# Two decode attentions on one core: the first K block ahead of B's query weights, and TensorE's loop rotated

## The chip, the cores and the metric

The kernel runs on one core of one Trainium2 chip. The metric is device time in microseconds (us) of one execution; lower is better. Before the change it takes 672.21 us (median of 3 runs, 672.11 to 673.36). One execution was also profiled: it took 671.92 us, and its trace spans 670.2 us from the first to the last instruction.

## The reference

Two independent one-token decode attentions, A and B, have the same sizes: D = 512, 32 heads of 128, a cache of 8192 keys and values per head, all bfloat16. Their outputs are put side by side.

```python
# for each of A and B; x is [1, 1, 512]
q = (x @ wq).reshape(1, 1, 32, 128).transpose(0, 2, 1, 3)
scores = einsum("bhqd,bhkd->bhqk", q, k_cache) * 128 ** -0.5
p = softmax(scores, axis=-1)
o = einsum("bhqk,bhkd->bhqd", p, v_cache)
y = o.transpose(0, 2, 1, 3).reshape(1, 1, 4096) @ wo      # [1, 1, 512]
# out = concatenate([y of A, y of B], axis=-1)
```

Each cache is 64 MiB, and there are four. Each of the four weight matrices is 4 MiB. Each of these bytes is read once.

## The kernel before, in words

**Groups.** Four heads make a group, so A has groups 0 to 7 and B has groups 8 to 15 (N = 16). K of a group (8 MiB) fills one of two SBUF buffers, `kn[0]` and `kn[1]`, in turn. V of a group (8 MiB) fills the only V buffer, `vn`. The query weights `wq` of A and of B (4 MiB each) also lie in `vn`, one half each, before V of group 0 overwrites them.

**One group.** VectorE multiplies K by the query, broadcast over the keys, in four blocks h = 0 to 3 (L307, `plan_mul`). For each block TensorE adds up groups of products with 16 matmuls against the identity into PSUM (L461, `scores`), and VectorE reduces these to 64 scores per partition (L312, `plan_sr`). After block 3 come the maximum (L319), two small matmuls on TensorE that turn it and broadcast it (L499, L502), and four exponentials on ScalarE (L335). PV is 256 matmuls (L490) and a small one for the sum of the exponentials (L483); VectorE scales the result (L341, L342).

**Queries.** The query of A is 32 matmuls (L277) once `wq` of A has landed, and that of B 32 more once `wq` of B has landed. ScalarE copies the results to `qbc`. In the code before, TensorE runs both sets before its loop begins.

**The loads.** SyncE (SP) issues every large load from one queue, in the order in which the program lists them: `wq` of A, `wq` of B, K of 0, K of 1, V of 0, K of 2, V of 1, K of 3, and so on. A load that must wait for a buffer holds up everything behind it. V of 0 waits for the last query matmul (`q_done`). V of n waits for PV of n-1 (`pv_done`). K of n+2 waits until the fourth score block of group n has been added up by TensorE (`red_done(n, 3)`). At the end come `wo` of A, the first half of `wo` of B, V of 15 in two parts, and the rest of `wo` of B in five smaller pieces, which land last.

**TensorE's program.** All engines but TensorE run straight code. TensorE has a real loop over r = 0 to 16 (L475), whose body is made of branches on r. In the order of the code: score blocks 0 to 2 of group r, in two copies, one for each K buffer (L470, L476); for r = 16 alone the middle part, that is the relayout, the output product of A, and the first half of that of B (L478); for r > 0 PV of group r-1 (L480); for r < 16 block 3 of group r and the two small matmuls (L496), and back to the top (L475). After the loop follows the last part: the rest of B's output product, and its turn into rows (L419, L436). A part that a round does not use is jumped over. Register waits (`_Stepped`) count up round by round.

So from one round to the next TensorE does: blocks 0 to 2 of group r, PV of r-1, block 3 of group r, small matmuls, then blocks 0 to 2 of r+1.

Of the kernel before, what the change touches and what calls it, by code (L numbers as in the profile page):

```python
# [11 lines left out]
P = 128  # L12
# [11 lines left out]
class _Plan:  # L24
# [15 lines left out]
    def op(self, eng, fn, ctr=None, needs=(), inc=1):  # L40
        for m in needs:
            self.wait(eng, m)
        self.prog[eng].append((fn, ctr, inc))
        if ctr is None:
            return None
        ctr.n += inc
        return ctr, ctr.n


def _emit(e, items):  # L50
    for fn, ctr, k in items:
        if fn is None:
            e.wait_ge(ctr.sem, k)
        elif ctr is None:
            fn(e)
        else:
            fn(e).then_inc(ctr.sem, k)
# [18 lines left out]
def bass_concat_heads__mha_block_cached__gqa_block_cached__decode_kernel(  # L76
# [16 lines left out]
    wqs = [A_wq, B_wq]  # L93
    wos = [A_wo, B_wo]
    NA = 2
# [7 lines left out]
    G = 4  # L103
    HP = P // G
    T = Sk // HP
    assert T == 256
    GA = H // G
    N = NA * GA
    NB = 4
    HT = T // NB  # L110
    DW = 512 // HT
    VT = 192
# [7 lines left out]
    with ExitStack() as st:  # L120
# [3 lines left out]
        def sb(name, shape, dt):  # L124
            return ec(nc.sbuf_tensor(name, shape, dt))

        kn = [sb("k%d" % i, [P, T, Dh], BF16) for i in range(2)]
        vn = sb("vn", [P, T, Dh], BF16)
# [3 lines left out]
        wq_buf = [vflat[:, a * WQ:(a + 1) * WQ] for a in range(NA)]  # L132
# [5 lines left out]
        pt = sb("pt", [P, T, G], BF16)  # L138
# [4 lines left out]
        ones_f = sb("ones_f", [P, P], F32)  # L143
        ident = sb("ident", [P, P], BF16)
        ident_f = sb("ident_f", [P, P], F32)
        m1 = sb("m1", [P, 1], F32)
        gm = sb("gm", [1, G], F32)
        gmx = sb("gmx", [1, P], F32)
        negb = sb("negb", [P, N], F32)
        rsum = sb("rsum", [P, G], F32)  # L150
# [10 lines left out]
        def ps(name, shape):  # L161
            return ec(nc.psum_tensor(name, shape, F32))

        rps = ps("rps", [P, 2, 512])
        acc = ps("acc", [P, 512])
        mtp = ps("mtp", [P, 512])
        bmp = ps("bmp", [P, 512])
        misc = ps("misc", [P, 512])
        yps = [ps("yps%d" % i, [P, 512]) for i in range(2)]

        pl = _Plan()
        op, wait = pl.op, pl.wait

        def ctr(name):
            return _Ctr(nc, st, name)

        s_x = ctr("s_x")
        s_w = [ctr("s_w%d" % a) for a in range(NA)]
# [3 lines left out]
        s_v, s_v2 = ctr("s_v"), ctr("s_v2")  # L182
# [3 lines left out]
        c_red, c_sum, c_pv, c_gx, c_bc = ctr("c_red"), ctr("c_sum"), ctr("c_pv"), ctr("c_gx"), ctr("c_bc")  # L186


        def red_done(n, h):
            return c_red, NB * n + h + 1  # L190
# [13 lines left out]
        def dma(eng, dst, src, c, needs=()):  # L204
            return op(eng, lambda e: e.dma_start(dst, src), c, needs, inc=16)  # L205


        def const(fn, needs=()):
# [12 lines left out]


        x_in = [dma("ACT", xrow[0:1, a, :], xs[a][0], s_x) for a in range(NA)][-1]
        wq_in = [dma("SP", wq_buf[a], wqs[a].rearrange("(p c) n -> p (c n)", p=P), s_w[a])
                 for a in range(NA)]
        k_in, v_in = {}, {}

        def load_k(n):
            a, i = divmod(n, GA)
            src = ks[a][0, G * i:G * (i + 1)].rearrange("h (p t) d -> (h p) (t d)", p=HP)  # L230
            k_in[n] = dma("SP", kflat[n % 2], src, s_k[n % 2],
                          [red_done(n - 2, NB - 1) if n >= 2 else None])
# [8 lines left out]
        def load_wob(g, need=None):  # L241
# [9 lines left out]
                dst = wo_sb[1][:, h0:h0 + n, :]  # L251
            wob_in.append(dma("SP", dst, src, s_wob[g], [need]))


        def xmm(e):
            r = None
            for a in range(NA):
                for c in range(C):
                    k = (a * C + c) * HP
                    r = e.matmul(misc[:, k:k + HP], xrow[0:1, a, c:D:C], ones_bf[0:1, 0:HP],  # L260
                                 start=True, stop=True)
            return r
        m = op("PE", xmm, c_pe, [x_in, i_pool])
# [2 lines left out]
        y_free = [x_ready, x_ready]  # L266
        qbc_ready = {}
        q_done = None
        for a in range(NA):
            for j in range(GA // 4):  # L270
                def qmm(e, a=a, j=j):
                    r = None
                    for hh in range(G):
                        for c in range(C):
                            w = wq_sb[a][:, c, 16 * j * Dh:16 * (j + 1) * Dh].rearrange(
                                "p (i h d) -> p i h d", h=G, d=Dh)[:, :, hh, :]
                            r = e.matmul(  # L277
                                yps[j % 2][hh * HP:(hh + 1) * HP, :].rearrange("p (i d) -> p i d", d=Dh),
                                xb[:, a, c, :], w, start=(c == 0), stop=(c == C - 1))
                    return r  # L280
                q_done = op("PE", qmm, c_pe, [x_ready, wq_in[a], y_free[j % 2]])
                n0 = a * GA + 4 * j
                y_free[j % 2] = op("ACT", lambda e, n0=n0, j=j: e.copy(
                    qbc[:, n0:n0 + 4, :].rearrange("p i d -> p (i d)"), yps[j % 2][:]), c_act, [q_done])
                for n in range(n0, n0 + 4):
                    qbc_ready[n] = y_free[j % 2]
# [56 lines left out]
                oD[:, a, G * i:G * (i + 1)], acc[:, 0:G], rinv[:, n, :], ALU.mult),  # L343
                c_o, [pv_done(n), m])

        load_k(0)
        load_k(1)
        for n in range(N):
            if n < N - 1:
                load_v(n, pv_done(n - 1) if n else q_done)  # L350
# [27 lines left out]
        mid0 = len(pl.prog["PE"])  # L378
# [29 lines left out]
        m = op("PE", mm_a, c_pe, [o2_ready[0, 0], woa_in, y_free[0]])  # L408
        m = op("ACT", lambda e: e.copy(out_a[:], yps[0][0:1, :]), c_act, [m])
# [19 lines left out]
        mid1 = len(pl.prog["PE"])  # L429
# [3 lines left out]
        for g in range(NPRE, len(WOB)):  # L433
            m = mm_b(g)
        m = op("DVE", lambda e: e.tensor_copy(yT[:], yps[1][:, 0:NQ]), c_dve, [m])
        m = op("PE", lambda e: e.matmul(bmp[0:NQ, 0:P], yT[:], ident[:], start=True, stop=True),  # L436
               c_pe, [m, p_done[N - 1]])
        m = op("DVE", lambda e: e.tensor_copy(out_b[:], bmp[0:NQ, 0:P]), c_dve, [m])
# [5 lines left out]

        def pe_program(e):
            prog = pl.prog["PE"]
            _emit(e, prog[:mid0])
            w_mul = _Stepped(e, c_mul, 1, 1)
            w_sr = _Stepped(e, c_sr, SR0 - 1, 1)
            w_g = _Stepped(e, c_g, 1, 1)  # L450
            w_o = _Stepped(e, c_o, O0, 1)
            w_p = _Stepped(e, c_p, G, G)
            w_v = _Stepped(e, s_v, 16, 16)

            def scores(slot, hs):
                for h in hs:
                    w_mul.wait()
                    w_sr.wait()
                    r = None
                    for i in range(Dh // DW):  # L460
                        r = e.matmul(  # L461
                            rps[:, h % 2, :].rearrange("p (t d) -> p t d", d=DW), ident[:],
                            kn[slot][:, h * HT:(h + 1) * HT, i * DW:(i + 1) * DW],
                            start=(i == 0), stop=(i == Dh // DW - 1))
                    r.then_inc(c_red.sem, 1)
                    w_mul.grow()
                    w_sr.grow()

            def scores_of(r, hs):
                with e.If(r % 2 == 0):  # L470
                    scores(0, hs)
                with e.Else():
                    scores(1, hs)

            with e.Fori(0, N + 1) as r:  # L475
                with e.If(r < N):  # L476
                    scores_of(r, range(0, NB - 1))
                with e.If(r == N):  # L478
                    _emit(e, prog[mid0:mid1])
                with e.If(r > 0):  # L480
                    w_o.wait()
                    w_p.wait()
                    e.matmul(misc[:, 0:G], ones_f[:], rsum[:], start=True, stop=True).then_inc(c_sum.sem, 1)  # L483
                    w_v.wait()
                    m = None
                    for t in range(T):
                        if t == VT:
                            with e.If(r == N):
                                e.wait_ge(s_v2.sem, 16)
                        m = e.matmul(acc[:, 0:G], vn[:, t, :], pt[:, t, :],  # L490
                                     start=(t == 0), stop=(t == T - 1))
                    m.then_inc(c_pv.sem, 1)
                    w_o.grow()
                    w_p.grow()
                    w_v.grow()
                with e.If(r < N):  # L496
                    scores_of(r, range(NB - 1, NB))
                    w_g.wait()
                    e.matmul(mtp[0:1, 0:P], m1[:], ident_f[:], start=True, stop=True).then_inc(c_gx.sem, 1)  # L499
                    w_g.grow()  # L500
                    w_g.wait()
                    e.matmul(bmp[:, 0:1], gmx[:], ones_f[0:1, 0:1], start=True, stop=True).then_inc(c_bc.sem, 1)  # L502
                    w_g.grow()
            _emit(e, prog[mid1:])

        for name, at in (("SP", block.sync), ("PE", block.tensor), ("ACT", block.scalar),
                         ("DVE", block.vector), ("POOL", block.gpsimd)):
# [34 lines left out]
```

## Time and profile before

| what | number |
|---|---|
| median of 3 runs | 672.21 us |
| the profiled execution: its time, its span | 671.92 us, 670.2 us |
| read from HBM | 285.21 MB, 426 GB/s over the span |
| TensorE matmuls busy | 439.5 us (66%) |
| VectorE busy | 342.6 us (51%) |
| ScalarE busy | 62.2 us (9%) |
| first K block landed, VectorE's first multiply | 42.02 us |
| first PV begins | 94.89 us |

A busy TensorE is not a full one: matmuls are pipelined, and their ends are modelled. The DMA figures are of all 16 DMA engines together. In the chain of work, each row is a piece of the chain that ended last, with its start, its length and what it was. "issue" there is time in which an engine waited for nothing that the profile names. In rows that list one source line, `PEldq` means the sequencer of TensorE, which hands its instructions out, and the three durations are the shortest, the median and the longest, in ns.

### The profile page before, as it was taken

The page shows a single profiled execution, that of the slowest core. Times are in us where ns is not written, and L with a number is a line of the kernel's source. Part 1 is how long each engine was busy: PE and PEld are TensorE (multiplying, and loading weights), DVE is VectorE, ACT ScalarE, POOL GpSimd, SP SyncE. Part 2 cuts the span into 40 slices and gives each one's busy share as a digit, 9 for nine tenths or more (in the row PEclk, how much of TensorE's full clock was granted, in tenths as well). Part 3 has the DMA queues.
Part 4 walks back from the last instruction along what each step waited for, and adds up shares of the span by engine and source line. Part 5 has one row for each costly group of instructions (what it writes and reads, how often), then busy time and mean ns, then how long its engine had stood idle before and what let it go on. Part 6 is the DMA issues. An engine that isn't in the chain of part 4 may idle for free.

```text
span 670.2 us, 11845 instructions
## 1 busy us (share of the span) xinstructions
PE 439.5 (66%) x5453; PEld 241.9 (36%) x5453; DVE 342.6 (51%) x229; ACT 62.2 (9%) x151; POOL 2.0 (0%) x10
## 2 busy tenths in 40 slices
PE   2225696969577584948759483865938387694877
PEld 1002252525235261513426161442616144261626
DVE  1046565657292735629183663909266380836520
ACT  1100202020200102020100202020020201002020
POOL 1000000000000000000000000000000000000000
PEclk9659797979777676978776697877658796676886
DMA  9999999999999999999999999999999999999996
GB/s 376 438 438 429 435 391 375 438 438 439 438 434 438 434 426 396 438 438 438 438 438 438 438 438 438 430 438 430 426 411 430 438 438 434 438 438 438 406 448 278
DMA packets 6198, 285.33 MB, mean 426 GB/s; under 512 B 683, under 2 KB 1198, under 8 KB 1326
## 3 DMA queue, kind: packets, MB, share of 16 engines
q1 hardware_dynamic: 6184, 285.22, 98.7%
q8 instruction: 5, 0.08, 0.1%
q14 instruction: 3, 0.02, 0.0%
q10 hardware_dynamic: 6, 0.00, 0.0%
HBM read 285.21 MB, written 0.00 MB: 426 GB/s over the span
## 4 chain that ended last, share of the span: by engine, by line
DMA 60%; PE 27%; DVE 11%; issue 1%; SPq 0%
DMA vn<-in_B_v_cache_dram 19%; PE rps L461 15%; DMA k<-in_B_k_cache_dram 14%; DMA k<-in_A_k_cache_dram 13%; PE acc L490 12%; DVE k L307 10%; DMA vn<-in_A_v_cache_dram 9%; DMA k<-in_B_wo_dram 4%; DVE s_sb L312 1%; SPq L205 0%; DVE m L319 0%; PE mtp L499 0%; DVE gm L320 0%; PE misc L483 0%; DVE gmx L323 0%
## 5 line engine op out<-in xcount | busy, mean ns | idle before, releaser
L461 PE MATMUL rps<-k,ident 128*128 128x512 bf16 x1024 | 296.2, 458 | 171.0 <-DVE k L307 163.3
L307 DVE TENSOR_TENSOR k<-k,qbc 128x8192 bf16<-128x8192 bf16 x64 | 281.4, 4418 | 94.7 <-DMA k<-in_A_k_cache_dram 57.0
L461 PEld LDWEIGHTS rps<-k,ident 128*128 128x128 bf16 x1024 | 112.5, 114 | 342.8 <-DVE k L307 173.3
L312 DVE TENSOR_REDUCE s_sb<-rps 128x64 f32<-128x512 f32 x64 | 44.1, 689 | 196.2 <-PE rps L461 196.2
L490 PE MATMUL acc<-pt,vn 128*128 128x4 bf16 x4096 | 108.9, 165 | 6.1 <-DMA vn<-in_B_v_cache_dram 3.8
L490 PEld LDWEIGHTS acc<-pt,vn 128*128 128x128 bf16 x4096 | 108.2, 100 | 7.0 <-DMA vn<-in_B_v_cache_dram 4.3
L335 ACT ACTIVATE pt<-s_sb,negb 32x256 bf16<-32x256 f32 x64 | 54.8, 856 | 1.9
L328 ACT ACTIVATE negb<-bmp 128x1 f32<-128x1 f32 x16 | 2.7, 171 | 560.1 <-PE bmp L502 560.1
L499 PE MATMUL mtp<-ident_f,m 128*1 128x128 f32 x32 | 6.1, 271 | 19.8 <-DVE m L319 19.8
L335 ACT ACTIVATION_READ_ACCUMULATOR pt<-s_sb,negb 32x1 f32 x64 | 15.9, 248 | 0.0
L277 PE MATMUL yps<-vn,xb 128*32 128x512 bf16 x64 | 7.3, 630 | 10.6 <-DMA vn<-in_B_wq_dram 6.0
L502 PE MATMUL bmp<-ones_f,gmx 1*128 1x1 f32 x32 | 6.2, 259 | 9.9 <-DVE gmx L323 9.9
L499 PEld LDWEIGHTS mtp<-ident_f,m 128*1 128x1 f32 x32 | 1.4, 81 | 27.7 <-DVE m L319 27.7
L502 PEld LDWEIGHTS bmp<-ones_f,gmx 1*128 1x128 f32 x32 | 4.8, 186 | 14.6 <-DVE gmx L323 14.6
L405 PE MATMUL yps<-k,o 128*1 128x512 bf16 x32 | 8.4, 429 | 0.0
L320 DVE TENSOR_REDUCE gm<-mtp 1x4 f32<-1x128 f32 x16 | 4.4, 278 | 7.5 <-PE mtp L499 7.5
L341 DVE RECIPROCAL rinv<-misc 128x4 f32<-128x4 f32 x16 | 2.8, 174 | 10.1 <-PE misc L483 10.1
L277 PEld LDWEIGHTS yps<-vn,xb 128*32 128x32 bf16 x64 | 2.7, 134 | 14.3 <-issue 7.5
L342 DVE TENSOR_TENSOR oD<-acc,rinv 128x4 bf16<-128x4 f32 x16 | 2.6, 163 | 9.7 <-PE acc L490 8.1
L319 DVE TENSOR_REDUCE m<-s_sb 128x1 f32<-128x256 f32 x16 | 6.7, 420 | 0.5
L483 PEld LDWEIGHTS misc<-rsum,ones_f 128*128 128x128 f32 x32 | 6.0, 190 | 2.2
L260 PE MATMUL misc<-ones_bf,xrow 1*128 1x32 bf16 x8 | 0.4, 192 | 8.0 <-DMA xrow<-in_B_x_dram 8.0
(35 smaller groups left out, 32.5 us busy)
## 6 DMA issues: line engine op xcount, KB each, us to landing
vn<-in_B_v_cache_dram SPq DMA_DIRECT2D x1, 6144.0 KB, 22.3
vn<-in_A_wq_dram SPq DMA_DIRECT2D x1, 4096.0 KB, 12.2
vn<-in_B_wq_dram SPq DMA_DIRECT2D x1, 4096.0 KB, 21.4
k<-in_A_wo_dram SPq DMA_DIRECT2D x1, 4096.0 KB, 35.8
k<-in_B_wo_dram SPq DMA_DIRECT2D x1, 2048.0 KB, 40.3
vn<-in_B_v_cache_dram SPq DMA_DIRECT2D x1, 2048.0 KB, 26.8
k<-in_B_wo_dram SPq DMA_DIRECT2D x1, 1024.0 KB, 28.8
k<-in_B_wo_dram SPq DMA_DIRECT2D x1, 512.0 KB, 29.6
```

The source lines that it names most:

```text
L277: r = e.matmul(yps[j % 2][hh * HP:(hh + 1) * HP, :].rearrange("p (i d) -> p i d", d=Dh), xb[:, a, c, :], w, start=(c == 0), stop=(c == C - 1))
L307: mul_done[n, h] = op("DVE", lambda e: e.tensor_tensor(k, k, qbc[:, n:n + 1, :].broadcast_to([P, HT, Dh]), ALU.mult), c_mul, [k_in[n], qbc ...
L312: sr_done[n, h] = op("DVE", lambda e: e.tensor_reduce(s_sb[:, h * HT:(h + 1) * HT], rps[:, h % 2, :].rearrange("p (t d) -> p t d", d=DW), ...
L319: op("DVE", lambda e: e.tensor_reduce(m1[:], s_sb[:], AX.X, ALU.max), c_g)
L320: m = op("DVE", lambda e: e.tensor_reduce(gm[:], mtp[0:1, 0:P].rearrange("o (h p) -> o h p", h=G), AX.X, ALU.max), c_dve, [gx_done(n)])
L335: p_done[n] = op("ACT", lambda e, h=h, q=q: e.activation(pt[q, :, h], s_sb[q, :], AF.Exp, bias=negb[q, n:n + 1], scale=scale, accum_out=rs ...
L405: r = e.matmul(yps[0][0:1, :], o2[:, 0, j:j + 1], wo_sb[0][:, j, :], start=(j == 0), stop=(j == H - 1))
L461: r = e.matmul(rps[:, h % 2, :].rearrange("p (t d) -> p t d", d=DW), ident[:], kn[slot][:, h * HT:(h + 1) * HT, i * DW:(i + 1) * DW], star ...
L483: e.matmul(misc[:, 0:G], ones_f[:], rsum[:], start=True, stop=True).then_inc(c_sum.sem, 1)
L490: m = e.matmul(acc[:, 0:G], vn[:, t, :], pt[:, t, :], start=(t == 0), stop=(t == T - 1))
L499: e.matmul(mtp[0:1, 0:P], m1[:], ident_f[:], start=True, stop=True).then_inc(c_gx.sem, 1)
L502: e.matmul(bmp[:, 0:1], gmx[:], ones_f[0:1, 0:1], start=True, stop=True).then_inc(c_bc.sem, 1)
```

## The change: what it does

1. The list of SP's loads begins `wq` of A, K of 0, `wq` of B, K of 1. The rest is as it was.
2. TensorE runs only A's query ahead of its loop. B's 32 query matmuls are emitted inside the loop, for r = 0 alone, after score blocks 0 to 2 of group 0.
3. The loop body is rotated. Its order in the code is now: block 3 and the small matmuls of group r-1 (`scores_end`, for 0 < r <= 16), blocks 0 to 2 of group r (r < 16), B's query (r = 0), the middle part (r = 16), the last part (r = 17), PV of group r-1 (0 < r <= 16). The loop runs to r = 17, and the last part lies inside it, ahead of PV.

Apart from B's query the order in which TensorE executes its work is the same; VectorE, ScalarE and GpSimd have the same instructions in the same order.

```diff
-        wq_in = [dma("SP", wq_buf[a], wqs[a].rearrange("(p c) n -> p (c n)", p=P), s_w[a])
-                 for a in range(NA)]
-        k_in, v_in = {}, {}
+        wq_in, k_in, v_in = {}, {}, {}
+
+        def load_wq(a):
+            wq_in[a] = dma("SP", wq_buf[a], wqs[a].rearrange("(p c) n -> p (c n)", p=P), s_w[a])
...
+        load_wq(0)
+        load_k(0)
+        load_wq(1)
+        load_k(1)
...
+        q0 = None
         for a in range(NA):
+            q0 = len(pl.prog["PE"])
             for j in range(GA // 4):
...
-        load_k(0)
-        load_k(1)
         for n in range(N):
...
-            _emit(e, prog[:mid0])
+            _emit(e, prog[:q0])
...
-            def scores_of(r, hs):
-                with e.If(r % 2 == 0):
-                    scores(0, hs)
+            def pv(r):
...
+            def scores_end(r):
+                with e.If(r % 2 == 1):
+                    scores(0, range(NB - 1, NB))
                 with e.Else():
-                    scores(1, hs)
-
-            with e.Fori(0, N + 1) as r:
+                    scores(1, range(NB - 1, NB))
+                w_g.wait()
+                e.matmul(mtp[0:1, 0:P], m1[:], ident_f[:], start=True, stop=True).then_inc(c_gx.sem, 1)
+                w_g.grow()
+                w_g.wait()
+                e.matmul(bmp[:, 0:1], gmx[:], ones_f[0:1, 0:1], start=True, stop=True).then_inc(c_bc.sem, 1)
+                w_g.grow()
+
+            with e.Fori(0, N + 2) as r:
+                with e.If(r > 0):
+                    with e.If(r <= N):
+                        scores_end(r)
                 with e.If(r < N):
-                    scores_of(r, range(0, NB - 1))
+                    with e.If(r % 2 == 0):
+                        scores(0, range(0, NB - 1))
+                    with e.Else():
+                        scores(1, range(0, NB - 1))
+                with e.If(r == 0):
+                    _emit(e, prog[q0:mid0])
                 with e.If(r == N):
                     _emit(e, prog[mid0:mid1])
+                with e.If(r > N):
+                    _emit(e, prog[mid1:])
                 with e.If(r > 0):
...
-            _emit(e, prog[mid1:])
+                    with e.If(r <= N):
+                        pv(r)
```

`pv` holds the lines that stood at L481 to L495, unchanged.

More of the change, by code (lines that the diff above doesn't have):

```diff
@@ L467, in scores @@
                     w_sr.grow()
-            def scores_of(r, hs):
-                with e.If(r % 2 == 0):
-                    scores(0, hs)
-                with e.Else():
-                    scores(1, hs)
-            with e.Fori(0, N + 1) as r:
-                with e.If(r < N):
-                    scores_of(r, range(0, NB - 1))
+            def pv(r):
+                w_o.wait()
+                w_p.wait()
+                e.matmul(misc[:, 0:G], ones_f[:], rsum[:], start=True, stop=True).then_inc(c_sum.sem, 1)
+                w_v.wait()
+                m = None
+                for t in range(T):
+                    if t == VT:
+                        with e.If(r == N):
+                            e.wait_ge(s_v2.sem, 16)
+                    m = e.matmul(acc[:, 0:G], vn[:, t, :], pt[:, t, :],
+                                 start=(t == 0), stop=(t == T - 1))
+                m.then_inc(c_pv.sem, 1)
+                w_o.grow()
+                w_p.grow()
+                w_v.grow()
@@ L480, in pe_program @@
                 with e.If(r > 0):
[L481 to L503, printed above, removed]
```

## The prediction, made before the changed kernel was run

> **What bounds the kernel now.** I read the page's slices and queues first, then the stages, then the chain of waits from its start, then single rows of TensorE's sequencer.
>
> ```profile
> span 670.2 us, 11845 instructions
> ...
> GB/s 376 438 438 429 435 391 375 438 438 439 438 434 438 434 426 396 438 438 438 438 438 438 438 438 438 430 438 430 426 411 430 438 438 434 438 438 438 406 448 278
> ...
> q1 hardware_dynamic: 6184, 285.22, 98.7%
> q8 instruction: 5, 0.08, 0.1%
> ```
>
> Each slice is 16.8 us. Nearly all move 438 GB/s, and 285 MB at that rate are 651 of the 670 us: the loads are the bound, and only time in which they stand still can be won. They do in the first slice (start), the last (tail), and slices 5 and 6 (391, 375). The stages around these:
>
> ```profile
> 68.50:106.50 38.00, 30.40 (x338) 15.91 (x337) 20.83 (x11) 3.61 (x9) 0.00 (x0) 0.78 0.93 394
> 106.50:150.00 43.50, 30.21 (x339) 15.83 (x338) 29.15 (x19) 7.23 (x18) 0.00 (x0) 0.81 1.00 434
> ```
> ```profile
> 99.00:100.00 1.00, 1.00 (x44) 1.00 (x41) 0.00 (x0) 0.00 (x0) 0.00 (x0) 0.50 0.16 66
> 100.00:101.00 1.00, 1.00 (x43) 1.00 (x41) 0.00 (x0) 0.00 (x0) 0.00 (x0) 0.50 0.15 66
> 101.00:102.00 1.00, 0.88 (x25) 0.67 (x23) 0.00 (x0) 0.00 (x0) 0.00 (x0) 0.50 0.00 0
> 102.00:103.00 1.00, 1.00 (x4) 0.31 (x3) 0.00 (x0) 0.00 (x0) 0.00 (x0) 0.50 2.36 786
> ```
>
> The last column is GB/s. Against 434 the first stage lost 38.0 x (1 - 394/434) = 3.5 us, and the second table puts it at 99 to 102: the queue was empty. SP's issues tell why.
>
> ```profile
> 26.41 0.33 SPq L205 DMA_DIRECT2D vn<-in_A_v_cache_dram  x1
> 73.35 0.33 SPq L205 DMA_DIRECT2D k<-in_A_k_cache_dram  x1
> 101.66 0.33 SPq L205 DMA_DIRECT2D vn<-in_A_v_cache_dram  x1
> 107.36 0.33 SPq L205 DMA_DIRECT2D k<-in_A_k_cache_dram  x1
> 135.72 0.33 SPq L205 DMA_DIRECT2D vn<-in_A_v_cache_dram  x1
> ```
>
> These are V of 0, K of 2, V of 1, K of 3, V of 2. V of 1 waits for PV of 0, which comes so late that all before it has landed. Traffic restarts in 102 to 103, about 1 us after that issue. So whatever moves PV of 0 by s us earlier wins min(s, 3.5), and whatever moves it later costs as much. The chain up to it:
>
> ```profile
> 42.02 4.44 DVE k L307
> ...
> 62.41 0.61 DVE s_sb L312
> 63.02 4.84 issue
> 67.86 5.48 PE rps L461 x16
> ...
> 75.50 4.35 DVE k L307
> ...
> 95.03 6.59 PE acc L490 x256
> 101.63 0.12 issue
> ```
>
> Group 0 starts when its K lands (42.02). Its block 3 begins on TensorE at 67.86, after 4.84 us in which nothing named was awaited. VectorE runs in order, so group 1's multiplies (75.50) and PV of 0 follow from 67.86 at a fixed distance: 101.62 - 67.86 = 33.8 us to the end of PV. The 4.84 us are a branch:
>
> ```profile
> L480 PEldq COMPARE_BRANCH  x17: 68/77/8927, 58.4 to 655.5; - x17
> L478 PEldq COMPARE_BRANCH  x18: 71/206/354, 58.0 to 655.2; - x18
> L475 PEldq COMPARE_BRANCH  x17: 67/208/214, 75.8 to 664.3; - x17
> ```
>
> The jump over PV in round 0 (L480, at 58.4) took 8.93 us, to 67.3; its median is 0.08. Instruction packets went with it. Of the five of the whole run, one fell in 51 to 52, two in 62.9 to 63.9, one in 72.5 to 73.5, one in 665.5 to 666.5; here the rows of the second and the third:
>
> ```profile
> q8 instruction: 2, 0.03, 22.3%
> ```
> ```profile
> q8 instruction: 1, 0.02, 6.6%
> ```
>
> So the code is loaded in pieces of 0.08 MB / 5 = 16 KB, each once, and a first jump into a piece that isn't there waits about 9 us under full DMA load; afterwards the same jump is free, and so is the loop's return (L475, 214 ns at most).
>
> **How much a piece holds.** I number TensorE's instructions from the code: two per matmul (weight load, multiply; four for float32), one per wait, branch and register step. Before: slot-0 blocks at 162 to 264, middle part 369, PV's test 573, block 3 1095, last part 1181 to 1313. The jump 264 to 573 cost 0.35 us at most (L478), 573 to 1095 the 8.93. Packets come some 4.7 us after what asks for them (58.4 to about 63.1). The one in 51 to 52 was therefore asked for near 46.5, when the first score block was released and the sequencer stood near 195; the last one on entering the part at 1181 to 1313. Four pieces lie between, so one holds some 250 (estimate), and each is asked for on entering the one ahead of it. Starts, estimated: 195, 450, 705, 960, 1220, that is pieces 1 to 5.
>
> [...]
>
> **The change, part by part.**
>
> *K of 0 ahead of `wq` of B.*
>
> ```profile
> 13.09 3.64 PE L277 MATMUL yps<-vn,xb 128*32 128x512 bf16 x32 [4.61 <-DMA vn<-in_A_wq_dram]
> 22.68 3.64 PE L277 MATMUL yps<-vn,xb 128*32 128x512 bf16 x32 [5.95 <-DMA vn<-in_B_wq_dram]
> ```
>
> `wq` of B takes 22.68 - 13.09 = 9.6 us of the loads, so K of 0 lands 9.6 us earlier, at 32.4, and block 2's matmuls, which ran
>
> ```profile
> 57.53 3.63 PE L461 MATMUL rps<-k,ident 128*128 128x512 bf16 x16 [1.66 <-DVE k L307]
> ```
>
> run at 47.9 to 51.6. The bytes ahead of V of 1 stay the same, so the queue runs dry at the same 99 us unless V of 1 comes earlier. By itself this part would bring PV of 0 forward by 9.6 us and win the whole 3.5.
>
> *B's query after block 2.* `wq` of B lands at about 42, so it doesn't wait. 32 matmuls cost 3.64 us above on a TensorE that had stood idle, perhaps half right behind other matmuls (block 2 took 3.63 for 16, the first ones after idle 5.48). It ends at 53.5 to 55.2. V of 0, then issued at about 54 instead of 26.41, still comes before K of 1 is through:
>
> ```profile
> 1.73 40.27 DMA k<-in_A_k_cache_dram
> ...
> k<-in_A_k_cache_dram SPq DMA_DIRECT2D x2, 50.5
> ```
>
> (from issue to landing; 50.5 is the median of K of 0, 40.3, and K of 1, so 60.7 for the latter: landed at about 62.9). Cost nothing, 8 us of cover. K of 2, behind V of 0 on SP's queue, waits for block 3 at 73.35, later than that in either case. ScalarE's copies for B end long before its first exponential.
>
> *The rotated loop in round 0.* Positions now: `scores_end` 98 to 178, slot-0 blocks 182 to 284, B's query 389 to 454, test for the middle part 455, for the last part 660, for PV 794, loop end 1317. Piece 1 is entered in block 0 and asks for piece 2 early. The sequencer runs ahead of the array by up to 16 matmuls (L480 began at 58.4 with block 2's matmuls running to 61.16), so it leaves B's query at about 52.5. There it enters piece 2 (450) and only now asks for piece 3. The jump 455 to 660 is within piece 2 (0.35). The jump 660 to 794 needs piece 3: a wait. The test at 794 jumps to 1317, in piece 5, skipping piece 4: a second wait, of the same kind as L480's. Then back to the top, which is there.
>
> Price of a wait: none of these can be seen in before except the one of 8.93. That one had two packets; 22.3% of 16 engines over 1 us is 3.6 us for both, against 6.6% or 1.1 us for one alone, so the longer of two took 1.8 to 2.5. One packet alone makes it 8.0 (8.93 less about 0.95). First wait 8.0, second 8.9, together 16.9. Bounds: both waits overlap to one, 8.9, below; two of 9.5, 19, above. I take 16.9, since the second can't be asked for before the test at 794 has been read.
>
> Return, by the medians around 0.1 to 0.2 us a test (L475, L480), seven instructions: 1.0. Block 3 then starts at 52.5 + 0.35 + 16.9 + 1.0 = 70.75, against 67.86: PV of 0 ends 2.9 us later, V of 1 is issued at 104.6, and the gap grows from 3.5 to 6.4. K of 2 goes out at 76.2, still ahead of the end of V of 0 (26.41 + 57.3 = 83.7 landed):
>
> ```profile
> vn<-in_A_v_cache_dram SPq DMA_DIRECT2D x1, 57.3
> ```
>
> *Later rounds.* Each now has the loop's return and four more tests between PV and block 3, about 0.5 us more. It delays V and K loads by as much, but from 106.5 on the queue never empties (434); V of 2 was issued at 135.72, K of 3 landed at 107.36 + 35.6 = 143.0:
>
> ```profile
> k<-in_A_k_cache_dram SPq DMA_DIRECT2D x1, 35.6
> ```
>
> Cover of about 5 us there, growing, since a group takes VectorE and TensorE 33.9 us (block 3 at 67.86, the next at 101.75) and the loads 16.8 MB / 0.434 = 38.7. Cost nothing.
>
> *The tail.*
>
> ```profile
> 657.43 6.97 PE L490 MATMUL acc<-pt,vn 128*128 128x4 bf16 x256 [1.36 <-DMA vn<-in_B_v_cache_dram]
> ...
> 664.82 1.01 PE L419 MATMUL yps<-o,k 128*128 128x1 bf16 x32 [0.42 <-DMA k<-in_B_wo_dram]
> 666.11 0.59 PE L419 MATMUL yps<-o,k 128*128 128x1 bf16 x16 [0.28 <-DMA k<-in_B_wo_dram]
> 666.88 0.82 PE L419 MATMUL yps<-oD,k 128*128 128x1 bf16 x16 [0.18 <-DMA k<-in_B_wo_dram]
> ```
>
> The last part waited for pieces of `wo`. Now some nine tests, five of them taken, lie between PV and it: about 1.9 us, start at 665.9 instead of 664.82. Its 64 matmuls need about 1.9 us without waits, to 667.8 against 667.7. I take +0.2, bounds 0 and 0.7.
>
> Sum: +2.9 + 0.2 = +3.1 on 671.92, that is 675.0; the profiled execution is 0.3 below the median, so 675.3 against 672.21. I say 675.2.
>
> **Rivals.** *One wait only.* If the piece at 794 is there in time, or both requests run together, block 3 starts at 52.85 + 8.9 + 1.0 = 62.8, 5 us earlier; the gap closes: 672.2 - 3.5 + 0.2 = 668.9, and no more, as the gap holds no more. For it: two packets came together at 62.9 to 63.9, so requests can overlap. Against: after one wait the jump over PV still leaves piece 3 for piece 5. It decides where both waits together stay under 12.5 us. *The change hides itself.* With 12.5 to 15.2 us of waits, what K's order wins the second wait takes, 672 within 1.3. *B's query delays V of 0.* If it ended after about 61 the loads would pause there; 672.2 plus the delay, say 677. It would need 7 us more than reckoned.
>
> **How the numbers follow.** About 0.2% (1.3 us) is what a measurement of this kernel can tell from no change. Two waits: 0.57 (own range 673.6 to 677). Hides itself: 0.15. One wait or none: 0.26. V of 0 late: 0.02. Slower 0.59, same 0.15, faster 0.26. The range goes from the one-wait case, 668.5, to two waits of 9.5, 677.3.
>
> **What would show it.** Right: a branch of some 8 us at the last part's test and one of some 9 us at PV's, both in round 0; one instruction packet, then two; first multiply at 32.4; block 3 near 71; V of 1 issued near 104.6; a gap of 6 us. Wrong: one long branch, block 3 before 66, no gap at 99 us.

## The result, and the profile after

The changed kernel takes 675.87 us (median of 8 runs, 674.1 to 677.38), against 672.16 us for the kernel before beside it (8 runs). The ratio is 1.0057, 95% interval 1.0041 to 1.0073: slower by about 3.7 us, and 675.2 was forecast. The profiled execution took 675.69 us, with a span of 673.9 against 670.2.

The page's slices of the changed kernel:

```profile
span 673.9 us, 11922 instructions
...
GB/s 374 435 438 435 433 381 311 436 436 436 436 436 436 436 436 436 436 436 436 436 436 436 436 432 436 436 436 432 436 436 428 432 432 424 428 432 428 422 439 252
...
q8 instruction: 5, 0.08, 0.1%
```

The hollow, the stretch in which the loads stand still, is again in slices 5 and 6 (counted from 0), and it is deeper (381 and 311, before 391 and 375). The stages around it, the last column being GB/s:

```profile
71.00:109.00 38.00, 29.77 (x338) 15.85 (x337) 20.83 (x11) 3.61 (x9) 0.00 (x0) 0.78 0.87 366
109.00:150.00 41.00, 27.94 (x336) 15.13 (x334) 26.24 (x18) 6.58 (x17) 0.00 (x0) 0.82 1.00 435
```
```profile
101.00:102.00 1.00, 1.00 (x45) 1.00 (x42) 0.00 (x0) 0.00 (x0) 0.00 (x0) 0.72 0.00 0
...
104.00:105.00 1.00, 0.25 (x9) 0.20 (x7) 0.00 (x0) 0.00 (x0) 0.00 (x0) 0.50 0.00 0
105.00:106.00 1.00, 1.00 (x3) 0.36 (x4) 0.00 (x0) 0.00 (x0) 0.00 (x0) 0.50 3.16 1049
```

The loads lost 38.0 x (1 - 366/435) = 6.0 us here, 3.5 before; nothing moved from 101 to 105. V of 0 went out at 55.04, K of 2 at 76.01, and V of 1 at 104.24 instead of 101.66:

```profile
55.04 0.33 SPq L205 DMA_DIRECT2D vn<-in_A_v_cache_dram  x1
76.01 0.33 SPq L205 DMA_DIRECT2D k<-in_A_k_cache_dram  x1
104.24 0.33 SPq L205 DMA_DIRECT2D vn<-in_A_v_cache_dram  x1
```

The start of the chain (start, length, what) follows, and then the sequencer's two tests that fall into it (L519 is the last part's, L521 is PV's):

```profile
33.63 4.44 DVE k L315
...
49.46 3.63 PE rps L467 x16
53.08 1.88 PE yps L285 x32
54.96 15.73 issue
70.68 5.31 PE rps L467 x16
...
97.61 6.60 PE acc L485 x256
104.21 0.75 issue
```
```profile
L519 PEldq COMPARE_BRANCH  x18: 77/208/6852, 53.9 to 669.4; - x18
L521 PEldq COMPARE_BRANCH  x18: 70/70/8662, 60.8 to 671.7; - x18
```

K of group 0 is there 8.4 us earlier than before, and B's query costs 1.88 us. Then TensorE stands for 15.73 us while its sequencer is in two jumps, 6.85 us from 53.9 and 8.66 us from 60.8, one behind the other. Everything won by the new order of the loads is spent there, and 2.8 us more.

### The profile page after: what moved, and what is told of

It is laid out like the page before. It is cut to its first block, busy times and chain, and to the rows that moved or that the text cites. A ratio compares the mean times of both kernels' runs of the same rounds, so it can differ in the third digit from the quotient of the medians.

```text
span 673.9 us, 11922 instructions
## 1 busy us (share of the span) xinstructions
PE 440.7 (65%) x5453; PEld 241.9 (36%) x5453; DVE 342.6 (51%) x229; ACT 62.3 (9%) x151; POOL 2.0 (0%) x10
## 4 chain that ended last, share of the span: by engine, by line
DMA 53%; PE 32%; DVE 11%; issue 4%; SPq 0%; DVEq 0%
DMA vn<-in_B_v_cache_dram 19%; PE rps L467 16%; DMA k<-in_B_k_cache_dram 13%; PE acc L485 13%; DMA k<-in_A_k_cache_dram 11%; DMA vn<-in_A_v_cache_dram 9%; DVE k L315 9%; PE yps L411 1%; DVE s_sb L320 1%; PE yps L425 1%; PE yps L285 0%; DVE m L327 0%; PE mtp L498 0%; DVE gm L328 0%; PE misc L478 0%
## 5 line engine op out<-in xcount | busy, mean ns | idle before, releaser
L467 PE MATMUL rps<-k,ident 128*128 128x512 bf16 x1024 | 299.3, 461 | 179.5 <-DVE k L315 153.7
L285 PE MATMUL yps<-vn,xb 128*32 128x512 bf16 x64 | 5.3, 487 | 4.8 <-DMA vn<-in_A_wq_dram 4.8
L291 ACT CAST qbc<-yps 128x512 bf16<-128x512 f32 x4 | 2.3, 585 | 44.5 <-PE yps L285 44.5
```

The lines of the kernel that those rows point to most:

```text
L285: r = e.matmul(yps[j % 2][hh * HP:(hh + 1) * HP, :].rearrange("p (i d) -> p i d", d=Dh), xb[:, a, c, :], w, start=(c == 0), stop=(c == C - 1))
L467: r = e.matmul(rps[:, h % 2, :].rearrange("p (t d) -> p t d", d=DW), ident[:], kn[slot][:, h * HT:(h + 1) * HT, i * DW:(i + 1) * DW], star ...
```

## The experiments

Each, but for the changed kernel itself, was run in 5 rounds beside the kernel before. V of 1's issue and the span are from the kernel's one profiled execution, the median from all its runs; the kernel before has 101.66 and 670.2.

| kernel | jumps over 3 us ahead of block 3 of group 0 | V of 1 issued | span | median us | ratio (95%) |
|---|---|---|---|---|---|
| changed | 6.9 + 8.7 | 104.24 | 673.9 | 675.87 | 1.0057 (1.0041 to 1.0073) |
| changed_again | 6.4 + 8.6 | 104.56 | 674.4 | 675.73 | 1.0064 (1.0050 to 1.0078) |
| last_outside | 8.1 | 97.61 | 667.5 | 669.28 | 0.9964 (0.9950 to 0.9978) |
| empty_round_after | none in the way | 89.41 | 666.2 | 669.16 | 0.9961 (0.9947 to 0.9976) |
| rotate_only | 5.9 + 8.8 | 110.03 | 678.4 | 680.98 | 1.0151 (1.0126 to 1.0176) |
| old_loop_order | 8.6 | 96.12 | 667.5 | 669.21 | 0.9963 (0.9948 to 0.9977) |
| order_alone | 9.3 | 100.06 | 668.5 | 669.46 | 0.9962 (0.9948 to 0.9975) |
| empty_round_before | none in the way | 97.04 | 667.6 | 669.36 | 0.9959 (0.9945 to 0.9972) |
| unrolled_plain | none, but PV of 0 is held up | 99.97 | 668.4 | 669.91 | 0.9960 (0.9946 to 0.9973) |
| unrolled_order | none, but PV of 0 is held up | 92.68 | 666.4 | 668.14 | 0.9940 (0.9926 to 0.9953) |
| dead_copy | 8.2 | 97.58 | 667.4 | 669.28 | 0.9965 (0.9952 to 0.9978) |
| dead_copy_kept | 6.8 + 8.9 | 104.09 | 672.5 | 674.44 | 1.0037 (1.0024 to 1.0051) |
| empty_round_last_outside | none in the way | 90.66 | 667.5 | 669.21 | 0.9969 (0.9957 to 0.9981) |

One line runs through the table. Wherever V of 1 goes out at 99.9 or later, the span is that issue plus 568.4 to 568.5 us: before, order_alone, unrolled_plain, dead_copy_kept, rotate_only. Only the changed kernel is above it, by 1.2 (1.4 in changed_again). Below about 98 an earlier issue brings nothing more; the spans stay at 666.2 to 667.6. What places a kernel within that band is not known: empty_round_after alone ran from 667.95 to 670.70 us. Each point of the line is one execution, and runs of one kernel can lie further apart (order_alone 668.72 to 670.41, rotate_only 679.39 to 684.06), so small steps between medians should not be read off it.

**last_outside: the last part back behind the loop.**

```diff
-            with e.Fori(0, N + 2) as r:
+            with e.Fori(0, N + 1) as r:
...
-                with e.If(r > N):
-                    _emit(e, prog[mid1:])
...
+            _emit(e, prog[mid1:])
```

> The changed kernel with its last part put back behind the loop, so that the test of PV in round 0 stands 133 instructions earlier, in a piece of code that is already there. Theory 'code pieces': one first-time jump is left, of 7 to 9 us; block 3 of group 0 starts at 62 to 63 us, the gap in the loads at 99 us closes, 669.0 us (668.5 to 670). Rival 'tests' (the rotated loop's extra tests and its return between PV and block 3 cost the time, round by round): they are all still there, 675. Rival 'order' (K ahead of wq of B upsets the loads): 675.

It took 669.28 us. Of its tests in round 0 one was long, PV's:

```profile
L518 PEldq COMPARE_BRANCH  x17: 77/77/8121, 54.3 to 654.5; - x17
```

Block 3 began at 63.52. The loads and the rotation are those of the changed kernel. Two tests `r <= N`, always true once the loop ends at r = 16, went out with the last part; dead_copy below has them again and takes the same 669.28. So both rivals fall: 133 instructions (counted from the code) between the middle part and PV, none of them executed in round 0, were the difference between 0.36% faster and 0.57% slower.

**empty_round_after: one round without work ahead of the others.** The loop runs over one round more, and each condition is shifted by one, for instance

```diff
-            with e.Fori(0, N + 2) as r:
-                with e.If(r > 0):
-                    with e.If(r <= N):
+            with e.Fori(0, N + 3) as r:
+                with e.If(r > 1):
+                    with e.If(r <= N + 1):
                         scores_end(r)
```

> The changed kernel with one round more at the front, in which no part runs: the sequencer only makes the tests and jumps, while K of group 0 is still on its way. Theory 'code pieces': two long branches, 7 and 9 us, fall between 18 and 36 us, where nothing waits for TensorE; in the round that counts no branch is longer than 0.4 us, block 3 of group 0 starts at about 55, the gap closes: 672.2 - 3.5 + 1.1 of the tail = 669.8 (669 to 671). 'Tests' and 'order': 675, since the same tests, loads and order are there.

It took 669.16 us. Three tests were long, all in the empty round, between 15 and 37 us, while K of 0 was on its way:

```profile
L516 PEldq COMPARE_BRANCH  x19: 69/206/6875, 15.4 to 661.2; - x19
L520 PEldq COMPARE_BRANCH  x19: 77/208/6707, 22.6 to 661.7; - x19
L522 PEldq COMPARE_BRANCH  x19: 70/70/7598, 29.4 to 664.0; - x19
```

One more than expected: the empty round comes to piece 2 before it has been fetched, which in the changed kernel happens unseen while TensorE waits for K (the packet falls at 19.6 there). Block 3 began at 55.83. The waits belong to the first visit of a piece of code, not to what round 0 does.

**rotate_only: the rotated loop, the old order of the loads, both queries ahead of the loop.**

```diff
         load_wq(0)
-        load_k(0)
         load_wq(1)
+        load_k(0)
         load_k(1)
...
-            _emit(e, prog[:q0])
+            _emit(e, prog[:mid0])
...
-                with e.If(r == 0):
-                    _emit(e, prog[q0:mid0])
```

> The rotated loop with the last part in it, but the loads in the old order and B's query ahead of the loop as before. Theory 'code pieces': two long branches again, 7 and 9 us from 58.4; block 3 at about 75, V of 1 issued near 109, the gap 7 us longer than before: 680 (678 to 681.5). 'Order': the old order is back, 672. 'Tests': 675.

It took 680.98 us. There were two long tests, 5.94 us from 59.9 and 8.79 us from 65.9, and block 3 began at 75.82:

```profile
L517 PEldq COMPARE_BRANCH  x18: 77/209/5937, 59.9 to 673.6; - x18
L519 PEldq COMPARE_BRANCH  x18: 70/70/8788, 65.9 to 676.2; - x18
```

So the rotated loop, with the last part in it, costs 1.5% by itself, and the new order in front of it hides more than half of that. A small part of this is not the jumps: the first multiply began at 43.42 instead of 42.02 (see the last section).

**old_loop_order: the new order and the move of B's query, in the loop as it was.**

```diff
                 with e.If(r < N):
                     scores_of(r, range(0, NB - 1))
+                with e.If(r == 0):
+                    _emit(e, prog[q0:mid0])
                 with e.If(r == N):
```

> The loop as it was before, with the new order of the loads and B's query in PV's place in round 0. Theory 'code pieces': one long branch of 8 to 9 us as in the kernel before; block 3 at about 62, the gap closes, 668.7 (668 to 669.5). 'Order': 675. 'Tests': without the rotation's tests 672 or less.

It took 669.21 us. There was one long test of 8.60 us, and ahead of it one of 2.17 us from 51.5, whose instruction packet fell in 51 to 52, so that its piece had been asked for before; block 3 began at 62.94. The first two parts of the change are a gain of 0.37%. The third turns it into a loss, and within the third it is the last part's place in the loop, as last_outside shows.

**order_alone: the new order of the loads, nothing else.** The loads as in the changed kernel, TensorE's program as before.

> The kernel before with the new order of the loads and nothing else: both queries stay ahead of the loop, so TensorE waits for wq of B (42 us) before it may begin with group 0. Block 0 starts at about 46 as before, the one long branch stays, block 3 near 66 to 68: 'code pieces' says 672 (670.5 to 673). 'Order': 675.

It took 669.46 us, so the expectation of 672 missed. TensorE's rows, and PV's test:

```profile
42.09 3.64 PE L285 MATMUL yps<-vn,xb 128*32 128x512 bf16 x32 [25.79 <-DMA vn<-in_B_wq_dram]
45.67 7.44 PE L467 MATMUL rps<-k,ident 128*128 128x512 bf16 x32
54.77 3.63 PE L467 MATMUL rps<-k,ident 128*128 128x512 bf16 x16 [1.66 <-DVE k L315]
65.50 5.98 PE L467 MATMUL rps<-k,ident 128*128 128x512 bf16 x16 [7.10 <-issue]
```
```profile
L486 PEldq COMPARE_BRANCH  x17: 68/77/9314, 55.6 to 654.1; - x17
```

Block 0 does start at about 46, as I had said. But VectorE had multiplied blocks 0 and 1 by then, so block 1 follows without a pause, and block 2 starts at 54.77 instead of 57.53. I had looked at the first start alone. The long jump (9.31 us) then begins at 55.6 instead of 58.4, and V of 1 goes out 1.6 us earlier. This smallest edit of all, four loads in another order, gains 0.38%, as much as the first two parts of the change together (0.37%).

**empty_round_before: an empty round ahead of the kernel before.** The conditions are shifted as above.

> The kernel before with one empty round at the front, as above; loads and order as before. Theory 'code pieces': the branch of 8.9 us falls before 42 us, where TensorE has nothing to do; block 3 of group 0 starts at about 62.5 right behind VectorE's multiply, 5 us earlier than in the kernel before, the gap closes: 668.7 (668 to 669.5). If the branch's 8.9 us were a wait for something else in round 0 (data, a semaphore), it would stay there: 672.

It took 669.36 us. The 8.9 us went along with the empty round (8.94 us from 31.7, and 6.77 from 24.9 at the middle part's test ahead of it); block 3 began at 66.17, since K of 0 itself was ready only at 45.05. The wait is not one for data of round 0.

**unrolled_plain and unrolled_order: round 0 written out ahead of the loop.** `turn` is the two small matmuls. The line that emits B's query is in unrolled_order alone, which has the new order of the loads.

```diff
+            scores(0, range(0, NB - 1))
+            _emit(e, prog[q0:mid0])
+            scores(0, range(NB - 1, NB))
+            turn()
-            with e.Fori(0, N + 1) as r:
+            with e.Fori(1, N + 1) as r:
```

> Round 0 written out ahead of the loop (blocks 0 to 2, B's query, block 3, the small matmuls), the loop from round 1 in the old form, the loads in the new order. Theory 'code pieces': no long branch ahead of block 3, which starts at about 54; PV of 0 then waits for V of 0 at 83.7, V of 1 is issued near 91, and no gap: 668.7 (668 to 669.5), no more than with one wait, since the gap holds only 3.5 us.

> Round 0 written out as above, but the loads in the old order and both queries ahead of everything. Theory 'code pieces': block 3 at about 62.5, the gap closes all the same: 668.7, so the new order of the loads adds nothing once the code is straight. If the order has a worth of its own, this one is slower than the one with the new order by over 1 us.

They took 668.14 us (unrolled_order) and 669.91 (unrolled_plain). unrolled_order, the new order with straight code, is the fastest kernel of the study, 0.60% faster than before. No test is long in either; block 3 began at 52.94 and 62.70. But PV of 0 now meets its own code for the first time. TensorE in unrolled_plain:

```profile
88.12 3.16 PE L500 MATMUL acc<-pt,vn 128*128 128x4 bf16 x120
91.81 3.51 PE L500 MATMUL acc<-pt,vn 128*128 128x4 bf16 x127 [0.53 <-issue]
99.54 0.40 PE L500 MATMUL acc<-pt,vn 128*128 128x4 bf16 x9 [4.22 <-issue]
```

127 matmuls lie between two stops, 254 instructions and one test, about the 250 that the prediction estimated for a piece. TensorE runs through such a piece in 3.5 us and waits 4.2 for the next. V of 1 so goes out at 99.97, not at 62.70 + 33.8 = 96.5, and the expectation that the order of the loads would be worth nothing here missed too: with it there is room for this stop (V of 1 at 92.68), without it there isn't. That unrolled_order also lies 1.1 us below last_outside, whose loads have no hollow either, was not expected, and its cause is open.

**changed_again, dead_copy, dead_copy_kept, empty_round_last_outside: the tail.** The tail is the time from the issue of V of 15 to that of the last output. The profiled changed kernel is 1.2 us above the line of the table. Its tail takes 672.29 - 637.73 = 34.56 us, before 668.56 - 635.12 = 33.44. The diff is that of dead_copy_kept; dead_copy leaves the condition r > N as it was, and empty_round_last_outside is empty_round_after with the last part behind the loop.

```diff
-            with e.Fori(0, N + 2) as r:
+            with e.Fori(0, N + 1) as r:
...
-                with e.If(r > N):
+                with e.If(e.snap(w_g.reg) > 1000):   # dead_copy: r > N, as it was
                     _emit(e, prog[mid1:])
...
+            _emit(e, prog[mid1:])
```

> The changed kernel with the last part kept inside the loop as code that no round runs (the loop ends at r = 16), and run from a second copy behind the loop. Round 0 keeps its two far jumps, so block 3 of group 0 stays near 70.7 and V of 1 near 104.2; only the return and the seven tests between the last PV and the last part are gone. If these cost the 1.1 us by which the profiled changed kernel was longer behind V of 15's issue, this one takes 674.8; if the lower granted clock there (0.67 for 0.84) cost them, it takes 675.7 like the changed kernel itself.

> The changed kernel once more, beside the one with the dead copy: 675.7. Its tail, from V of 15's issue to the last output DMA's issue, was 34.56 us against 33.44 before; if the loop's tests set that, it is 34.3 to 34.6 again, if the clock's phase set it, it may be 33.4 to 34.6.

> The empty round at the front, and the last part behind the loop: against the empty round with the last part inside (669.16 us) only the tail's return and tests are taken away. There the tail was 33.46 us, no longer than before, so the tests were hidden: 669.2 again, within 0.5. If they cost, 668.2.

> As the kernel with the dead copy, but the copy inside the loop now hangs on a register whose value the build can't know (it never gets there), so that the copy stays in the code between the middle part and PV. Theory 'code pieces': the two far jumps of round 0 are back, 6 to 7 and 8.6 us, block 3 of group 0 near 70.7, V of 1 near 104.3, so 674.7 to 675.8, not the 669.28 of the kernel without the copy. For the tail: no tests lie between the last PV and the last part; if these cost the 1.1 us, 674.8; if they were hidden, 675.7.

dead_copy missed its aim: no round can reach its copy, its trace has no row of the copy's test, and it was last_outside once more (669.28 again). dead_copy_kept has the copy, and the rows of its two tests:

```profile
L519 PEldq COMPARE_BRANCH  x17: 208/208/6832, 53.9 to 660.4; - x17
L521 PEldq COMPARE_BRANCH  x17: 70/70/8876, 60.8 to 660.7; - x17
```

The two jumps are back (6.83 and 8.88 us), block 3 begins at 70.81, V of 1 goes out at 104.09: for round 0 the mere presence of 133 unused instructions is settled twice. Its tail is 670.85 - 637.39 = 33.46 us, and it takes 674.44; changed_again's tail is 34.54. The last pieces of the two chains, the changed kernel first:

```profile
661.59 6.64 PE acc L485 x256
668.23 1.33 issue
669.57 1.87 PE yps L425 x64
```
```profile
640.17 29.49 DMA k<-in_B_wo_dram
669.67 0.05 issue
669.72 0.28 PE yps L425 x4
```

Without the tests the tail ends on the last piece of `wo`, as before; with them on TensorE. empty_round_last_outside shows no gain from the same edit (669.21 against 669.16), and empty_round_after and rotate_only, with all the tests, have tails of 33.46. So the tests cost only where the last PV is late already. In the changed kernel it is: it starts 661.45 - 637.73 = 23.72 us behind its load's issue, before 657.43 - 635.12 = 22.31. Nor does a late PV cost anything without the tests: in dead_copy_kept it is as late, 661.14 - 637.39 = 23.75, and the tail is that of before. It takes both. The granted clock (third column from the right) in the 10 us behind V of 15's issue, the changed kernel, then rotate_only:

```profile
637.73:647.73 10.00, 7.17 (x20) 2.52 (x20) 2.14 (x7) 0.18 (x2) 0.00 (x0) 0.67 1.04 444
```
```profile
643.36:653.36 10.00, 6.07 (x22) 2.37 (x22) 2.91 (x11) 1.66 (x5) 0.00 (x0) 0.83 1.04 444
```

It is 0.67 in changed_again and dead_copy_kept too, two others with a late PV, and in old_loop_order. But the clock was not varied by itself, so that it is what makes PV late is argued, not shown.

## Why the prediction was right

*The bound and the exchange.* Right: the loads are full but for one hollow, and it grows by a microsecond for each by which V of 1 goes out later; five kernels between 99.97 and 110.03 lie on one line.

*K of 0 earlier.* The first multiply was forecast for 32.4 and came at 33.63, so the lead is 8.4 us instead of 9.6 (see the last section). That this part by itself would win the whole 3.5 does not hold as it stands: in order_alone K is there at 32.37, but block 0 waits for B's query, and V of 1 goes out only 1.6 us earlier.

*B's query.* "Perhaps half" of 3.64 was 1.88. The sequencer left it at 53.5, not at 52.5; that is the later K. V of 0's issue at 55.04 cost nothing, as forecast.

*Two far jumps.* Right in number, place and kind: one instruction packet with the first, two with the second. The answers for 58 to 59 and for 65 to 66 us:

```profile
q8 instruction: 1, 0.02, 6.2%
```
```profile
q8 instruction: 2, 0.03, 23.4%
```

The first was priced at 8.0 and took 6.85, the second at 8.9 and took 8.66. Block 3 was forecast for 70.75 and came at 70.68, but this closeness is luck, since the errors nearly cancel: 1.0 us of later start and 0.2 of a longer return against 1.4 of shorter waits. The hollow was put at 6.4 and is 6.0.

*Pieces that stay.* In round 17 the jump over PV is made again, at L522, and takes 209 ns. The loop's return from there to the top, over some 1,200 instructions by the prediction's positions, took 240 ns at most in all rounds:

```profile
L506 PEldq COMPARE_BRANCH  x18: 67/209/240, 69.7 to 672.2; - x18
```

So code that had come once was not waited for again in this run: from 69.6 us on no test took over 240 ns, and the five instruction packets of the whole run (0.08 MB) began by 76 us (one in 19 to 21, one in 58 to 59, two in 65 to 66, one in 75 to 76).

*Later rounds.* Between PV and block 3 TensorE now stands 0.57 to 0.76 us in the rows of the chain instead of 0.12, about the 0.5 forecast. The loads stay full (435 from 109 on), so this costs nothing, as forecast.

*The tail.* This is the term that was mis-sized: it was put at +0.2 with an upper bound of 0.7, and +1.1 was measured. The 64 matmuls without waits took 1.87 us as reckoned, but I let PV end when it had ended before; it started 1.4 us later against its load, and the tests came on top. The profiled execution's 3.8 us is 2.6 of hollow and 1.1 of tail.

*The rivals.* "One wait only" was priced at 668.9: last_outside, which has just that, took 669.28. It was a true rival, and only the place of the last part in the code decided against it. "The change hides itself" was nearer than its chance of 0.15 says: it needed waits of 12.5 to 15.2 us, and they were 15.5 here and 15.0 in changed_again. What took the time clear of it here was the start of the waits, 1.0 us later than forecast, and the tail's 1.1.

## What to carry to other kernels

A branch skips the work of a part, not its code: here, a first jump into code that was never near cost 5.9 to 9.3 us, in the changed kernel with the DMA engines busy 98% and 93% of its two jumps' time; so count the instructions between test and target, and look for single long branch rows before turning a loop. What lies between two parts mattered even where it never ran (674.44 us in dead_copy_kept, 669.28 in dead_copy); a part used once belongs behind the loop. An empty first round, run while the engine has nothing to do, paid for these visits out of the way (669.16 us in empty_round_after), though the first K block can come later with it (first multiply at 45.05 instead of 42.02 in empty_round_before). Straight code took these jumps away too and left one stop in PV of 0 (3.4 us in unrolled_order, 4.2 in unrolled_plain); with the new order of the loads it was the fastest here. And try the plain reordering of the loads alone first: here it gained as much as all but the straight code.

## What the runs showed of the hardware that was not expected

- The first visits in all kernels, but for the one of 2.17 us, took 5.9 to 9.3 us: the jumps over PV 7.6 to 9.3, those over shorter parts 5.9 to 6.9. The jump over PV is also the last of its chain and mostly came with two packets, so which of these makes it dearer is open.
- An instruction packet goes with a later landing of the K block in flight. In the new order, without one ahead of it, the first multiply begins at 32.37 (order_alone, old_loop_order) or 32.43 (unrolled_order). With one, at 19.6 to 20.0 us, it is 33.6 to 34.0 (changed_again, last_outside, dead_copy, dead_copy_kept and the changed kernel), though one packet holds only one of 16 engines, for about 1 us (6.2% of 16 in a 1 us window). In the old order the kernel before begins at 42.02 without one, and rotate_only, with one, at 43.42. Their number alone does not decide: empty_round_after, with three, the last about 1 us ahead, begins at 33.93; where two of three fell into the same microsecond it is later still (empty_round_last_outside 35.40, empty_round_before 45.05). What ties the block to the packet was not shown.
- Straight code of short matmuls outran the fetch here: in unrolled_plain 254 instructions in 3.5 us, then a stop of 4.2 us; in unrolled_order a stop of 3.4 us ahead of the same last 9 matmuls.
